# Strassen's scheme for three of the four kinds of products of an attention and two-layer kernel

## The chip, the cores and the metric

The kernel runs on one core of a Trainium2 chip. The metric is device time in microseconds (us); lower is better. The core's engines are TensorE (PE in the profile, with its weight loads as PEld), VectorE (DVE), ScalarE (ACT), GpSimd (POOL) and SyncE (SP, which only issues transfers here). Each runs its own instructions in order; they wait for each other with semaphores.

## The reference

Chunk-local softmax attention over 8 batches, 8 heads, 576 tokens and a head size of 64, in chunks of 64 tokens; its output, as 4608 tokens of 512 numbers, goes through two layers:

```python
scores = scale * np.matmul(q_c, k_c.transpose(0, 1, 2, 4, 3))
attn = softmax(scores)
x = np.matmul(attn, v_c)            # as [4608, 512]
g = x @ w_gate                      # [4608, 1536]
silu = g * (1.0 / (1.0 + np.exp(-g)))
x = silu * (x @ w_val) @ w_out      # [4608, 512]
h = x @ w_in                        # [4608, 2048]
g = h * (1.0 / (1.0 + np.exp(-1.702 * h)))
out = g @ w_out2                    # [4608, 512]
```

The weights reach the kernel as the bits of float64 numbers.

## The kernel before

**Tiles.** The tokens are cut into nine blocks of 512 (four units of 128 each). d_ff is cut into tiles of 128: 12 in layer 1, 16 in layer 2. A float32 operand is split into a high and a low part of float32r (`split`: ScalarE copies the high part, VectorE or GpSimd subtracts it to get the low one), and each product is three matmuls, high by high, high by low and low by high (`mm3`, lines 211 to 214). All operands of the layers stand in SBUF in both parts.

**Stages.** Phase 1 takes the blocks through attention and layer 1, with all of layer 1's weights on chip (36 tiles of 4 KB a partition, tag `w`). For each f tile there are a gate product and a value product (`product`, 4 k tiles x 3 = 12 matmuls of 512 columns each), then `gate` and `times` on ScalarE and VectorE, `split_h`, and one tile later `y_step`: 12 matmuls into four PSUM banks that gather the block's output. The block's y goes to DRAM. Blocks 0 and 1 share the time in which weights arrive: block 0 runs through half of d_ff, block 1 through all of it, then block 0 through the rest. In the first two f tiles the products are made in halves of 256 tokens. Phase 2 loads y back (`y_load`) and takes the blocks through layer 2 in the same way (`product`, `gate`, `split_h`, `o_step`, whose matmuls are lines 422 to 424); a block has 192 matmuls in its input products and 192 in `o_step`. One block thus has 288 + 144 matmuls in layer 1 and 192 + 192 in layer 2.

**Weights.** `conv_part` turns float64 words into float32 with one ScalarE instruction and three on VectorE (lines 266, 269, 272), and `split` makes the parts, the low one on GpSimd. `conv_to` spreads this over the first 200 us and over the last block of phase 1, where layer 2's weights take the place of layer 1's.

**Attention** (`attend`) on a unit: 32 small matmuls, a maximum, eight exponentials, a sum, a reciprocal and a product with it, four transposes, 32 small matmuls (lines 304 to 337). Units are made ahead of the block that needs them, over all of phase 1.

**Order.** Every instruction group is an `op` with a rough duration and a priority (a slot number). `Program.emit` is a list scheduler over these durations: it fixes, before the kernel runs, the order of each engine's instructions; the op with the lowest priority goes first among those that could start soonest. All transfers are issued by SP in the order so found, loads at line 200 and stores at line 203.

## Time and profile before

| what | value |
|---|---|
| time, median of 3 runs | 1839.46 us (1839.08 to 1840.76) |
| span of the profiled execution | 1837.8 us |
| the profiled execution's own time | not given beside its span |
| TensorE busy | 1818.9 us (99%), 9920 matmuls |
| VectorE, ScalarE, GpSimd busy | 741.6, 627.5, 109.7 us |
| transfers | 94.37 MB on SP's queue, 51 GB/s over the span |

The span runs from the first to the last instruction of one profiled execution. Busy shares say how long an engine had some instruction in flight. The chain that ended last is followed back from the last instruction through whatever released each one. Tables of stretches give the busy time of every engine between two times, the granted TensorE clock as a fraction of 2.4 GHz and the transfers' share and rate.

### The profile page before, as it was taken

The page shows a single profiled execution, that of the slowest core. Times are in us where ns is not written, and L with a number is a line of the kernel's source. Part 1 is how long each engine was busy: PE and PEld are TensorE (multiplying, and loading weights), DVE is VectorE, ACT ScalarE, POOL GpSimd, SP SyncE. Part 2 cuts the span into 40 slices and gives each one's busy share as a digit, 9 for nine tenths or more (in the row PEclk, how much of TensorE's full clock was granted, in tenths as well). Part 3 has the DMA queues.
Part 4 walks back from the last instruction along what each step waited for, and adds up shares of the span by engine and source line. Part 5 has one row for each costly group of instructions (what it writes and reads, how often), then busy time and mean ns, then how long its engine had stood idle before and what let it go on. Part 6 is the DMA issues. An engine that isn't in the chain of part 4 may idle for free.

```text
span 1837.8 us, 24124 instructions
## 1 busy us (share of the span) xinstructions
PE 1818.9 (99%) x9920; PEld 1476.0 (80%) x9920; DVE 741.6 (40%) x1246; ACT 627.5 (34%) x1208; POOL 109.7 (6%) x117
## 2 busy tenths in 40 slices
PE   8999999999999999999999999999999999999999
PEld 7777888888888878887888778888888888888887
DVE  7886333333333333333358863232323232323222
ACT  6663333233333332332335542222222222222222
POOL 2442000000000000000013320000000000000000
PEclk9999999999999999999999999999999999999999
DMA  8511121011101111011023521010101010100000
GB/s 327 207 41 41 58 63 42 24 58 29 46 30 35 46 29 50 32 29 47 29 92 125 162 80 47 0 47 0 46 1 47 1 46 1 46 1 35 1 23 24
DMA packets 47342, 95.91 MB, mean 52 GB/s; under 512 B 5248, under 2 KB 14464, under 8 KB 47232
## 3 DMA queue, kind: packets, MB, share of 16 engines
q1 hardware_dynamic: 47232, 94.37, 15.4%
q8 instruction: 78, 1.28, 0.3%
q14 instruction: 32, 0.26, 0.0%
HBM read 74.42 MB, written 19.92 MB: 51 GB/s over the span
## 4 chain that ended last, share of the span: by engine, by line
PE 84%; DVE 7%; issue 3%; ACT 3%; DMA 2%; POOL 0%; DVEq 0%; SPq 0%; ACTq 0%; POOLq 0%
PE g L212 16%; PE g L213 15%; PE g L214 15%; PE y L424 7%; PE y L423 7%; PE y L422 7%; PE y L212 5%; PE y L214 4%; PE y L213 4%; PE a L304 3%; DVE t L269 2%; DVE t L272 2%; DVE raw L266 1%; ACT t L264 1%; DMA w<-in_moe_w_val 1%
## 5 line engine op out<-in xcount | busy, mean ns | idle before, releaser
L363 DVE TENSOR_TENSOR h<-h,g 128x512 f32<-128x512 f32 x358 | 245.8, 686 | 753.4 <-ACT h L366 662.1
L366 ACT ACTIVATE h<-g 128x512 f32<-128x512 f32 x251 | 150.0, 598 | 643.8 <-PE g L214 643.1
L212 PE MATMUL g<-xbh,w 128*128 128x512 f32 x736 | 289.0, 393 | 0.8 <-DVE h L363 0.7
L213 PE MATMUL g<-xbl,w 128*128 128x512 f32 x736 | 287.6, 391 | 0.1
L214 PE MATMUL g<-xbh,w 128*128 128x512 f32 x736 | 286.6, 389 | 0.0
L212 PE MATMUL g<-xah,w 128*128 128x512 f32 (+1 forms) x704 | 279.4, 397 | 0.0
L214 PE MATMUL g<-xah,w 128*128 128x512 f32 (+1 forms) x704 | 277.7, 394 | 0.0
L213 PE MATMUL g<-xal,w 128*128 128x512 f32 (+1 forms) x704 | 277.5, 394 | 0.0
L206 ACT CAST hh<-h 128x512 fp32r<-128x512 f32 x252 | 156.4, 621 | 266.1 <-DVE h L363 265.7
L424 PE MATMUL y<-w,hl 128*128 128x512 f32 x576 | 229.2, 398 | 0.9 <-DVE hl L209 0.9
L422 PE MATMUL y<-w,hh 128*128 128x512 f32 x576 | 224.5, 390 | 1.5 <-DVE e L380 1.5
L423 PE MATMUL y<-w,hh 128*128 128x512 f32 x576 | 225.6, 392 | 0.0
L209 DVE TENSOR_TENSOR hl<-h,hh 128x512 fp32r<-128x512 f32 x246 | 169.7, 690 | 126.8 <-ACT hh L206 126.3
L212 PE MATMUL y<-hh,w 128*128 128x512 f32 x432 | 175.2, 406 | 0.2 <-PE y L457 0.2
L213 PE MATMUL y<-hl,w 128*128 128x512 f32 x432 | 169.9, 393 | 0.0
L214 PE MATMUL y<-hh,w 128*128 128x512 f32 x432 | 169.9, 393 | 0.0
L212 PEld LDWEIGHTS g<-xbh,w 128*128 128x128 f32 x736 | 138.1, 188 | 32.8 <-DVE h L363 2.4
L214 PEld LDWEIGHTS g<-xbh,w 128*128 128x128 f32 x736 | 138.2, 188 | 29.6
L213 PEld LDWEIGHTS g<-xbl,w 128*128 128x128 f32 x736 | 138.2, 188 | 29.5 <-DVE xbl L209 0.4
L212 PEld LDWEIGHTS g<-xah,w 128*128 128x128 f32 x704 | 132.9, 189 | 31.5 <-DVE h L363 0.5
L209 POOL TENSOR_TENSOR w<-t,w 128x256 fp32r<-128x256 f32 (+1 forms) x104 | 100.1, 964 | 968.8 <-ACT w L206 932.3
L214 PEld LDWEIGHTS g<-xah,w 128*128 128x128 f32 x704 | 132.9, 189 | 31.1
(84 smaller groups left out, 1645.7 us busy)
## 6 DMA issues: line engine op xcount, KB each, us to landing
e<-y_dram SPq DMA_DIRECT2D x36, 256.0 KB, 3.0
raw<-in_moe_w_out SPq DMA_DIRECT2D x36, 255.8 KB, 2.6
q<-in_q SPq DMA_DIRECT2D x32, 256.0 KB, 2.7
k<-in_k SPq DMA_DIRECT2D x32, 256.0 KB, 3.0
v<-in_v SPq DMA_DIRECT2D x32, 256.0 KB, 2.8
raw<-in_moe_w_in SPq DMA_DIRECT2D x32, 255.8 KB, 2.6
y_dram<-raw SPq DMA_DIRECT2D x28, 256.0 KB, 2.4
w<-in_moe_w_gate SPq DMA_DIRECT2D x11, 511.8 KB, 7.5
```

The costliest lines, as they stand in the source:

```text
L206: op("act", ((61 if psum else 112) + n) / 1.2e3, lambda: nc.scalar.copy(out=hi.ap, in_=src.ap), [src], [hi], prio)
L209: op(eng, us, lambda: e.tensor_tensor(out=lo.ap, in0=src.ap, in1=rd(hi.ap), op=ALU.subtract), [src, hi], [lo], prio)
L212: nc.tensor.matmul(o, ah, bh, start=first, stop=False)
L213: nc.tensor.matmul(o, ah, bl, start=False, stop=False)
L214: nc.tensor.matmul(o, al, bh, start=False, stop=last)
L269: op("dve", (66 + n) / 0.96e3, lambda: nc.vector.scalar_tensor_tensor(out=t.ap.bitcast(I32), in0=t.ap, scalar=-4096 * up, in1=word(1).bitc ...
L304: nc.tensor.matmul(o[r, of_o(i)], st[r, of_st(i)], mv[r, of_o(i)], start=True, stop=True)
L363: op("dve", 0.61, lambda: nc.vector.tensor_tensor(out=h.ap, in0=h.ap, in1=g.ap, op=by), [h, g], [h], prio)
L366: op("act", 0.48, lambda: nc.scalar.activation(out=h.ap, in_=g.ap, func=AF.Sigmoid, scale=by), [g], [h], prio, "sig")
L422: nc.tensor.matmul(os_[t].ap, gh.ap[:, ts], wh.ap, start=first, stop=False)
L423: nc.tensor.matmul(os_[t].ap, gh.ap[:, ts], wl.ap, start=False, stop=False)
L424: nc.tensor.matmul(os_[t].ap, gl.ap[:, ts], wh.ap, start=False, stop=last)
```

## The change

The two layers are done in five passes over all nine blocks: three for layer 1 (4 of its 12 f tiles each) and two for layer 2 (8 of 16). A pass has two groups of f tiles. For a group, the gate and value products (layer 1: two f tiles, so a 512 x 256 weight block for each of the two) or the input products (layer 2: four f tiles, as two such blocks) are made by Strassen's scheme, one level, in Winograd's form with seven products: the weight block and the block's x (512 x 512 tokens) are each cut in two both ways, and seven combinations of either side are multiplied, 12 matmuls of 256 columns for each combination and group. The seven partial products are added up on VectorE into `c`. The products with `wo` and `wo2` (`second`) stay as they were, 12 matmuls of 512 columns for each f tile.

What goes with it:

- Combinations of x: in pass 0 they are made from attention's output (`x_made`, four VectorE sums, seven splits on ScalarE and GpSimd) and stored to DRAM with both parts; passes 1 and 2 load them (`x_load`, seven tiles of 4 KB a partition for each block). In pass 2, y is summed up and its combinations are made and stored in the same way (`x_to_dram`) for passes 3 and 4.
- Combinations of weights (`combos`, four GpSimd sums of 256 columns): the first pass makes them from the host's weights at the start; during each pass those of the next one are converted, combined, split and stored to DRAM (`group_to_dram`), and loaded at the change of the pass (`pass_from_dram`). The ring `w` has 24 tiles; a pass takes 18 or 22.
- `conv_part` has two ScalarE instructions and two on VectorE in place of one and three.
- The low part of h is always made on GpSimd (`gated`); before, VectorE made it but for the first slots.
- y of layer 1, and now the output of layer 2 too, is summed over the passes through DRAM (`block_sum`).
- All attention runs in pass 0, block by block, with one buffer each for q, k, v, its scores and its second PSUM bank. PSUM: in pass 0 the partial products have two banks, later four.
- `second`'s matmuls of a group are put between the next group's products (`put`). The planner's durations are set anew.

The diff, cut to its core:

```diff
-        ("w", 3 * NF1), ("xah", 1), ("xal", 1), ("xbh", 1), ("xbl", 1), ("h", 1), ("hh", 2), ("hl", 2),
...
+        ("w", 24), ("x", 8), ("c", 3), ("s1", 1), ("u", 1), ("h", 2), ("hh", 3), ("hl", 3),
+        ("q", 1), ("k", 1), ("v", 1), ("e", 2), ("m", 2), ("z", 2), ("xr", 1), ("xt", 3),
+        ("raw", 2), ("t", 3), ("st", 3), ("ws", 2), ("yv", 2))}
...
+        ("y0", 1), ("y1", 1), ("y2", 1), ("y3", 1), ("g", 2), ("s", 1), ("a", 1))})
...
+                if layer == 1:
+                    g.pairs = [[wg[f] for f in fs], [wv[f] for f in fs]]
+                    g.outs = [wo[f] for f in fs]
+                    g.name = "a%d" % fs[0]
+                else:
+                    g.pairs = [[wi[f] for f in fs[:2]], [wi[f] for f in fs[2:]]]
+                    g.outs = [wo2[f] for f in fs]
+                    g.name = "b%d" % fs[0]
...
+        op("act", act_us(n), lambda: nc.scalar.activation(
+            out=t.ap, in_=raw.ap[:, :, 2], func=AF.Relu, scale=up, bias=offset.ap[:, :1]), [raw, offset], [t], prio)
+        op("act", act_us(n), lambda: nc.scalar.activation(
+            out=word(1).bitcast(F32), in_=raw.ap[:, :, 2], func=AF.Relu, scale=up, bias=offset.ap[:, 1:]),
+           [raw, offset, t], [raw], prio)
...
+    def combos(t0, t1, prio):
+        def half(i):
+            return lambda ap: ap[:, i * 256:(i + 1) * 256]
+        s1, s2, s3, s4 = [ring["st"].new([P, 256]) for _ in range(4)]
+        a = half(0), half(1)
+        yield t0, a[0]
+        yield t0, a[1]
+        tt(s1, t1, t1, ALU.add, 256, prio, "pool", a[0], a[1])
+        tt(s2, s1, t0, ALU.subtract, 256, prio, "pool", of_b=a[0])
+        yield s2, lambda ap: ap
+        tt(s3, t0, t1, ALU.subtract, 256, prio, "pool", a[0], a[0])
+        yield s3, lambda ap: ap
+        yield s1, lambda ap: ap
+        tt(s4, t0, s2, ALU.subtract, 256, prio, "pool", of_a=a[1])
+        yield s4, lambda ap: ap
+        yield t1, a[1]
...
+    def group_from_host(g, prio):
+        W[g] = [ring["w"].new([P, 2, 2, 256], F32R) for _ in range(7)], [ring["w"].new([P, 2, 512], F32R) for _ in g.fs]
+        ts = []
+        for var in range(2):
+            ts.append([conv_tile((g.name, var, i), g.pairs[var][i], prio) for i in range(2)])
+            for i, (src, cut) in enumerate(combos(*ts[-1], prio)):
+                hi, lo = [W[g][0][i].part(lambda ap, c=c, var=var: ap[:, var, c]) for c in range(2)]
+                split(hi, lo, src, 256, prio + 0.1 * i, "pool", cut)
...
+    def token_combos(xb, prio):
+        def quarter(j, n):
+            return lambda ap: ap[:, 2 * j:2 * j + 2, n * HT:(n + 1) * HT]
+        b = [[quarter(j, n) for n in range(2)] for j in range(2)]
+        t1, t2, t4 = [ring["xt"].new([P, 2, HT]) for _ in range(3)]
+        tt(t1, xb, xb, ALU.subtract, 512, prio, of_a=b[0][1], of_b=b[0][0])
+        tt(t2, xb, t1, ALU.subtract, 512, prio, of_a=b[1][1])
+        t3 = Buf(lambda: b[0][1](xb.ap), None, None, xb)
+        op("dve", dve_us(512), lambda: nc.vector.tensor_tensor(
+            out=t3.ap, in0=b[1][1](xb.ap), in1=b[0][1](xb.ap), op=ALU.subtract), [xb, t1], [t3], prio)
+        tt(t4, t2, xb, ALU.subtract, 512, prio, of_b=b[1][0])
+        same = lambda ap: ap
+        return [(xb, b[0][0]), (xb, b[1][0]), (t2, same), (t3, same), (t1, same), (xb, b[1][1]), (t4, same)]
...
+    def x_made(b, prio):
+        X[0, b] = []
+        for i, (src, cut) in enumerate(token_combos(xr.pop(b), prio)):
+            x = ring["x"].new([P, 2, 2, HT], F32R)
+            X[0, b].append(x)
+            split(*[x.part(lambda ap, c=c: ap[:, c]) for c in range(2)], src, 512, prio + i, "pool" if b else ("dve", "pool")[i % 2], cut)
+            store(x_dram[0][:, b, i], Buf(lambda x=x: x.ap.rearrange("p c a t -> p c (a t)"), None, None, x), [xd[0][b][i]], prio + i + 2)
...
+    def x_load(p, b, prio):
+        layer = passes[p][0]
+        X[p, b] = []
+        for i in range(7):
+            x = ring["x"].new([P, 2, 2, HT], F32R)
+            X[p, b].append(x)
+            load(x.part(lambda ap: ap.rearrange("p c a t -> p c (a t)")), x_dram[layer - 1][:, b, i], prio + 2 * i, [xd[layer - 1][b][i]])
...
+    def x_to_dram(xb, b, prio):
+        for i, (src, cut) in enumerate(token_combos(xb, prio)):
+            hi, lo = [ring[t].new([P, 2, HT], F32R) for t in (("q", "k"), ("v", "e"))[i % 2]]
+            split(hi, lo, src, 512, prio + i, "pool", cut)
+            for c, s in enumerate((hi, lo)):
+                store(x_dram[1][:, b, i, c], Buf(lambda s=s: s.ap.rearrange("p a t -> p (a t)"), None, None, s), [xd[1][b][i].part(None)], prio + i + 2)
...
+            m_tags.extend(["g", "g"] if prio < start[1][0] else ["g", "s", "g", "a"])
+        m = ring[m_tags.pop(0)].new([P, 2, HT])
+        w, x = W[g][0][i], xs[i]
+        def fn():
+            for var in range(2):
+                for kk in range(2):
+                    ks, cs = slice(kk * P, kk * P + P), kk
+                    mm3(m.ap[:, var], w.ap[:, var, 0, ks], w.ap[:, var, 1, ks], x.ap[:, 0, kk], x.ap[:, 1, kk],
+                        kk == 0, kk == 1)
+        op("pe", GV, fn, [w, x], [m], prio)
+        return m
...
+        for i in range(7):
+            at_i = at(i)
+            m = product(g, xs, i, at_i)
+            if i == 0:
+                copy(s1, m, 512, at_i)
+            elif i == 1:
+                tt(q[0][0], s1, m, ALU.add, 512, at_i)
+            elif i == 2:
+                tt(u2, s1, m, ALU.add, 512, at_i)
+            elif i == 3:
+                tt(u3, u2, m, ALU.add, 512, at_i)
+            elif i == 4:
+                tt(q[0][1], u2, m, ALU.add, 512, at_i)
+                tt(q[1][1], u3, m, ALU.add, 512, at_i)
+            elif i == 5:
+                tt(q[0][1], q[0][1], m, ALU.add, 512, at_i)
+            else:
+                tt(q[1][0], u3, m, ALU.subtract, 512, at_i)
+            put(i)
+        return c
...
+        for i, var in ([(0, 0), (1, 0)] if g.layer == 1 else [(i, var) for var in range(2) for i in range(2)]):
+            h = ring["h"].new([P, 2, HT])
+            by = 1.0 if g.layer == 1 else 1.702
+            op("act", act_us(512), lambda h=h, i=i, var=var, by=by: nc.scalar.activation(
+                out=h.ap, in_=of(var)(c[i].ap), func=AF.Sigmoid, scale=by), [c[i]], [h], prio, "sig")
+            tt(h, h, c[i], ALU.mult, 512, prio, of_b=of(var))
+            if g.layer == 1:
+                tt(h, h, c[i], ALU.mult, 512, prio, of_b=of(1))
+            hh = ring["hh"].new([P, BT], F32R)
+            hl = ring["hl"].new([P, BT], F32R)
+            split(*[Buf(lambda s=s: s.ap.rearrange("p (n t) -> p n t", n=2), s.prev, s.before, s) for s in (hh, hl)],
+                  h, 512, prio, "pool")
+            hs.append((hh, hl))
...
+            s = ring["yv"].new([P, BT])
+            copy(s, ys[e], 512, prio, "act" if e % 2 else "dve")
+            yd[layer, b, e] = Buf(None)
+            store(dram, s, [yd[layer, b, e]], prio)
+            return
...
+        s = ring["yv"].new([P, BT])
+        load(s, dram, prio - 14, [yd[layer, b, e]])
+        if last and layer == 1:
+            if e == 0:
+                xr[b] = ring["xr"].new([P, KD, BT])
+            tt(xr[b].part(lambda ap: ap[:, e]), s, ys[e], ALU.add, 512, prio)
+            if e == KD - 1:
+                x_to_dram(xr.pop(b), b, prio + 3)
+            return
...
+                def put(i, tj=tj, n=n, step=step):
+                    while len(pend) > n * (6 - i) // 7:
+                        pend.pop(0)(tj + (i + 0.5) * step / 7)
+                c = group_products(g, xs, lambda i, tj=tj, step=step: tj + i * step / 7, put)
...
+                if p == 0 and b + 1 < NB:
+                    for u in range(2):
+                        w = UPB * (b + 1) + 2 * j + u
+                        at = t + (2 * j + u) * 7
+                        attend(w, "s", at, at - 10)
+                    if j == 1:
+                        x_made(b + 1, start[p][b + 1] - 12)
...
```

## Rows read from the trace of the kernel before

**Rows 1.** The page: busy time by engine, and the chain by engine.
```profile
PE 1818.9 (99%) x9920; PEld 1476.0 (80%) x9920; DVE 741.6 (40%) x1246; ACT 627.5 (34%) x1208; POOL 109.7 (6%) x117
...
PE 84%; DVE 7%; issue 3%; ACT 3%; DMA 2%; POOL 0%; DVEq 0%; SPq 0%; ACTq 0%; POOLq 0%
```

**Rows 2.** Table of stretches: us, busy by engine, granted clock, DMA share, GB/s.
```profile
200.00:400.00 200.00, 200.00 (x1339) 162.00 (x1338) 76.56 (x133) 72.38 (x146) 0.00 (x0) 1.00 0.16 52
```

**Rows 3.** Timeline of SP: a block's first output store, eight blocks apart.
```profile
1127.46 0.34 SPq L203 DMA_DIRECT2D out<-raw  x1
...
1832.89 0.33 SPq L203 DMA_DIRECT2D out<-raw  x1
```

**Rows 4.** Timeline of SP: first stores of y, block 0's second half and block 8.
```profile
270.38 0.92 SPq L203 DMA_DIRECT2D y_dram<-t  x2
...
1039.59 0.80 SPq L203 DMA_DIRECT2D y_dram<-e  x2
```

**Rows 5.** Timeline of PE: 256-column matmuls, in two products the third and the twelfth.
```profile
24.35 0.28 PE L214 MATMUL g<-xah,w 128*128 128x256 f32 x1
...
25.41 0.28 PE L214 MATMUL g<-xah,w 128*128 128x256 f32 x1
...
27.43 0.28 PE L214 MATMUL g<-xah,w 128*128 128x256 f32 x1
...
28.50 0.28 PE L214 MATMUL g<-xah,w 128*128 128x256 f32 x1
```

**Rows 6.** Timeline of PE: 512-column matmuls from the same x buffer, twenty starts apart.
```profile
204.07 0.39 PE L212 MATMUL g<-xah,w 128*128 128x512 f32 x1
...
208.73 0.39 PE L214 MATMUL g<-xah,w 128*128 128x512 f32 x1
```

**Rows 7.** Groups by shape: weight loads, busy us and mean ns of one.
```profile
L212 PEld LDWEIGHTS g<-xah,w 128*128 128x128 f32 x704 | 132.9, 189 | 31.5 <-DVE h L363 0.5
```

**Rows 8.** Groups by shape: elementwise work, busy us, mean ns of one, idle before.
```profile
L363 DVE TENSOR_TENSOR h<-h,g 128x512 f32<-128x512 f32 x358 | 245.8, 686 | 753.4 <-ACT h L366 662.1 <-PE g L214 87.2
L206 ACT CAST hh<-h 128x512 fp32r<-128x512 f32 x252 | 156.4, 621 | 266.1 <-DVE h L363 265.7
L366 ACT ACTIVATE h<-g 128x512 f32<-128x512 f32 x251 | 150.0, 598 | 643.8 <-PE g L214 643.1 <-POOL hl L209 0.4
L209 POOL TENSOR_TENSOR w<-t,w 128x256 fp32r<-128x256 f32 x72 | 56.1, 779 | 885.9 <-ACT w L206 854.3 <-issue 24.9 <-POOL w L209 3.4
L209 POOL TENSOR_TENSOR w<-t,w 128x512 fp32r<-128x512 f32 x32 | 44.1, 1380 | 82.9 <-ACT w L206 78.0 <-DMA w<-in_moe_w_gate 5.0
L272 DVE SCALAR_TENSOR_TENSOR t<-raw,t 128x256 int32<-128x256 int32 x72 | 39.8, 553 | 2.1
L312 DVE TENSOR_REDUCE m<-a 128x8 f32<-128x512 f32 x32 | 22.0, 689 | 9.6 <-PE a L304 9.6
```

**Rows 9.** Timelines of DVE and POOL: a small op alone, and one beside GpSimd.
```profile
58.11 0.17 DVE L323 TENSOR_SCALAR z<-z 128x8 f32<-128x8 f32 x1
...
73.47 1.28 DVE L323 TENSOR_SCALAR z<-z 128x8 f32<-128x8 f32 x1
...
73.43 1.29 POOL L209 TENSOR_TENSOR hl<-h,hh 128x512 fp32r<-128x512 f32 x1 [2.67 <-ACT hh L206]
```

**Rows 10.** Groups of VectorE by shape, from 50 to 120 us alone.
```profile
L272 DVE SCALAR_TENSOR_TENSOR t<-w,t 128x512 int32<-128x512 int32 x17 | 14.0, 828 | 0.3
...
L323 DVE TENSOR_SCALAR z<-z 128x8 f32<-128x8 f32 x3 | 2.6, 863 | 0.1
...
L313 DVE TENSOR_SCALAR m<-m 128x8 f32<-128x8 f32 x4 | 1.8, 438 | 0.0
```

**Rows 11.** Table of stretches as in rows 2: saturated loads, and a loaded VectorE.
```profile
25.00:30.00 5.00, 5.00 (x87) 4.60 (x87) 4.53 (x8) 3.58 (x7) 1.55 (x2) 1.00 1.04 402
50.00:120.00 70.00, 64.96 (x443) 51.72 (x440) 58.20 (x91) 46.46 (x84) 28.68 (x21) 0.98 0.44 162
```

**Rows 12.** Timeline of POOL: its first work on weights.
```profile
9.04 1.27 POOL L209 TENSOR_TENSOR w<-t,w 128x512 fp32r<-128x512 f32 x1 [7.69 <-ACT w L206]
```

More of the change, by code (lines that the diff above doesn't have):

```diff
@@ L259, in conv_part @@
-    def conv_part(raw, t, n, need):
+    class Group:
+        pass
+    passes = []
+    for layer, nf, per in ((1, NF1, 4), (2, NF2, 8)):
+        for f0 in range(0, nf, per):
+            gs = []
+            for j in range(2):
+                g = Group()
+                fs = list(range(f0 + j * per // 2, f0 + (j + 1) * per // 2))
+                g.fs = fs
+                if layer == 1:
[6 more added lines that the diff above has]
+                    g.name = "b%d" % fs[0]
+                g.layer = layer
+                gs.append(g)
+            passes.append((layer, gs))
@@ new lines, in attention_two_moe_kernel, with conv_load @@
+    NPASS = len(passes)
+    GV, YS = 1.42, 0.70
+    start = []
+    t = 0.0
+    for p, (layer, gs) in enumerate(passes):
+        start.append([])
+        for b in range(NB):
+            start[p].append(t)
+            t += sum(7 * GV + 4 * YS * len(g.fs) for g in gs) + (10.5 if p == 0 and b < NB - 1 else 0)
+    start.append([t])
+    raws = {}
+    def conv_load(key, src, prio, early):
+        src = src.bitcast(I16)
+        n = 1 if early else 2
+        raws[key] = [ring["w" if early else "raw"].new([P, 512 // n, 4], I16) for i in range(n)]
+        for i, raw in enumerate(raws[key]):
+            w = 2048 // n
+            load(raw.part(lambda ap, w=w: ap.rearrange("p c t -> p (c t)")[:, :w - 1]), src[:, i * w + 1:(i + 1) * w],
+                 prio, width=2)
@@ L260, in word, with conv_tile, conv_part @@
+    def conv_tile(key, src, prio):
+        if key not in raws:
+            conv_load(key, src, prio - 8, False)
+        t = ring["t"].new([P, 512])
+        rs = raws.pop(key)
+        n = 512 // len(rs)
+        for i, raw in enumerate(rs):
+            conv_part(raw, t.part(lambda ap, c=i * n: ap[:, c:c + n]), n, prio)
+        return t
+    def conv_part(raw, t, n, prio):
         def word(i):
@@ L432, in attention_two_moe_kernel @@
[L432 to L445 removed]
+        copy(xr[b].part(lambda ap: ap[:, :, ts]), o, 512, prio, cut=lambda ap: ap.rearrange("p (a t) -> p a t", a=NP))
@@ new lines, in second, with fn @@
+    def second(layer, w, hh, hl, ys, e, first, last, prio):
+        es = slice(e * P, (e + 1) * P)
+        def fn():
+            if layer == 1:
+                mm3(ys[e].ap, w.ap[:, 0, es], w.ap[:, 1, es], hh.ap, hl.ap, first, last)
+            else:
+                mm3(ys[e].ap, hh.ap[:, es], hl.ap[:, es], w.ap[:, 0], w.ap[:, 1], first, last)
+        op("pe", YS, fn, [w, hh, hl], [ys[e]], prio)
+    y_dram = pool["dram"].tile([P, KD, NT], F32, name="y_dram")
+    o_dram = pool["dram"].tile([P, KD, NT], F32, name="o_dram")
@@ L545, in attention_two_moe_kernel @@
-    o_step(*pend, slot)
+        op("pe", 0.22, lambda: nc.tensor.matmul(warm.ap[:, :P], ident.ap, ident.ap, start=True, stop=True), [warm], [], 9999)
+    g0, g1 = passes[0][1]
+    early = [((g.name, var, i), g.pairs[var][i]) for g in (g0, g1) for var in range(2) for i in range(2)]
+    for j, (key, src) in enumerate(early[:EARLY]):
+        conv_load(key, src, -52 + 2 * j, True)
+        raws[key][0].ap
+    tags = ("g", "s", "y1", "y2")
+    for u in range(UPB):
+        attend(u, tags[u], -40 + 4 * u, -54 + 4 * u)
@@ new lines, in attention_two_moe_kernel, with spread, flush @@
+    group_from_host(g0, -22)
+    x_made(0, -15)
+    outs_from_host(g0, 2)
+    group_from_host(g1, 0)
+    outs_from_host(g1, 8)
+    def spread(p):
+        if p + 1 >= NPASS:
+            return []
+        jobs = [j for g in passes[p + 1][1] for j in group_to_dram(g, 0)]
+        a = start[p][0] + (45 if p == 0 else 10)
+        z = start[p + 1][0] - 60
+        return [(a + (z - a) * i / len(jobs), j) for i, j in enumerate(jobs)]
+    pend = []
+    def flush(n):
+        for _ in range(min(n, len(pend))):
+            pend.pop(0)()
```

403 lines of the change are left out of this document (166 added, 237 removed).

## The prediction, made before the changed kernel was run

> **What bounds the kernel now.** The page's table of engines comes first: TensorE is busy 99% of the span, VectorE 40%, ScalarE 34%, GpSimd 6%, and the chain that ended last gives TensorE 84% [rows 1]. A busy TensorE need not be a working one, since matmuls overlap, so the table of stretches is next: from 200 to 400 us it is busy 200.00 of 200 us at granted clock 1.00, the 2.4 GHz level, with VectorE at 38% [rows 2]. There only fewer or cheaper matmuls can save time. Their rate comes from the output stores: the first store of a block is issued at 1127.46 us and that of the block eight later at 1832.89 [rows 3]. Between them stand 8 x 384 - 12 = 3060 matmuls of 512 columns (after the last block no next product is put ahead of its sums), so one takes 705.43 / 3060 = 0.2305 us. In layer 1 seven blocks lie between the two stores of [rows 4]: 769.2 us, of which 7 x 432 - 12 = 3012 matmuls take 694.3; the rest, 74.9 us, is 24 attention units, 3.12 us each.
>
> The span then splits so: 9 blocks x 816 = 7344 matmuls x 0.2305 = 1692.8 us; 32 attention units x 3.12 = 99.9 (the first block's four lie in the start); what is left, 45.1 us, is start and end.
>
> **Products.** Of the 816 matmuls of a block, 480 are gate, value and second-layer input products: 4320 in all, 995.8 us. Strassen makes seven block products of eight and cuts the moving side to 256 columns: 90 groups (five passes, nine blocks, two groups) x 7 x 12 = 7560 matmuls. The kernel before has 256-column matmuls of the same form in its first slots: nine starts apart take 1.06 us in one product and 1.07 in the next [rows 5], 0.1183 us each. In the same x buffer one of 512 takes (208.73 - 204.07) / 20 = 0.2330 [rows 6], so halving the columns costs 1.55% more per column, and on the kernel's mean rate a 256-column matmul comes to 0.2305 / 2 x 1.0155 = 0.117 us. 7560 x 0.117 = 884.5: a gain of 111.3 us. Nothing extra per column gives 871 (a gain of 125), the slower stretch's 0.1189 gives 899 (97); I take the scaled value, since the x tiles come to lie in eight buffers and not in that one.
>
> The rule that speaks against this: the Trainium skill ("TensorE: Matmul & The Clock Gate", Part 3, The mechanism) has a weight load run beside a matmul only where their row groups differ, and here every load takes all rows. By that rule a pair would cost load plus matmul, and the change would lose far more than it gains. The trace disagrees: loads that last 189 ns in the records [rows 7] stand between matmuls 118 ns apart.
>
> **Second products and attention** keep their count: 3024 x 0.2305 = 697.0 and 99.9 us. With 884.5 that is 1681.4, and with the old 45.1 for start and end 1726.5 us: the span if everything added is hidden.
>
> **What is added beside TensorE.** Each group now evacuates seven partial products: one copy on ScalarE, seven 128x512 adds on VectorE; then the gate (ScalarE), two products per h in layer 1 (VectorE), the high part (ScalarE) and the low part, which moves from VectorE to GpSimd. By rows a VectorE op of this size is 0.69, ScalarE 0.60 to 0.62, GpSimd 1.38, or 0.78 for 256 columns [rows 8]. Half a block of layer 1 gives TensorE 84 x 0.117 + 24 x 0.2305 = 15.4 us, of layer 2 20.9. So a block has 30.7 us in pass 1 and 2, 43.2 in pass 0 (four attention units more) and 41.8 in pass 3 and 4.
>
> VectorE in pass 0, per block: 22 group ops 15.2, attention 4 x 2.7 = 10.8 (three ops of 0.69 and three of 0.2), four sums for Strassen's x 2.8, two copies of y 1.4, a ninth of the next pass's weight conversion (12 tiles x 4 x 0.55) 2.9: 33.1 of 43.2. In pass 2: 15.2, four sums of y and four of x 5.5, a ninth of 16 tiles 3.9: 24.6 of 30.7. In pass 1 it is 21 of 30.7, in 3 and 4 under 21 of 41.8. GpSimd, which did 6% of the span, gets two low parts 2.8 x 2, seven x splits 9.7 and a ninth of some 52 weight ops 4.5 in pass 0, 19.8 of 43.2 (46%), and 20.5 of 30.7 (67%) in pass 2.
>
> Those two cannot run freely side by side. A VectorE scalar op on 8 columns takes 0.17 us when GpSimd is idle; the one at 73.47 us takes 1.28, to the end of the GpSimd subtraction that began at 73.43 [rows 9]. Between 50 and 120 us, GpSimd busy 41% and VectorE 83% [rows 11], the shift of the weight conversion (two SBUF operands) averages 0.83 and the small scalar ops 0.86 and 0.44 [rows 10], against 0.69 and 0.2. Scaled to GpSimd's share, 0.16 x 21 + 0.5 x 8 = 7 us make VectorE 40 of 43.2 in pass 0, and 0.22 x 19 = 4.3 make it 28.9 of 30.7 in pass 2: still under TensorE, but with little left. Lower: 0, as in [rows 2] at a third of the load. Upper: TensorE's idle share of 50 to 120 us, 5.04 of 70 us or 7.2% [rows 11], on the 8 x 43.2 + 9 x 30.7 = 622 us of these two passes: 45. And the chain behind a group's last product (0.69 + 0.60 + 2 x 0.69 + 0.62 + 1.38 = 4.7 us) is covered by a leftover second product and two products, about 4: at worst 0.6 x 90 = 54 more. I take 28 of 99: the 50 to 120 us stretch also waited for weights that were still coming, and the planner puts more products into a gap that it foresees.
>
> The Trainium skill ("SBUF — State Buffer", Who interferes with whom) says that a VectorE op with two SBUF inputs, or in a two-port mode, and a GpSimd op that reads SBUF exclude each other entirely. By that alone pass 2 would hold the pair for 19 x 0.6 + 20.5 = 32 of 30.7 us and end 12 us later. The trace agrees on the exclusion, but what remains of a held VectorE op after GpSimd's end is short.
>
> **Transfers.** All go through SP's queue, in order. Loads saturate at 402 GB/s [rows 11]. Pass 2 asks most per block: seven x tiles of 0.52 MB, four y loads and fourteen x stores of 0.26 MB and a ninth of 16 weight tiles in and 44 halves out: 10.6 MB in 30.7 us, 345 GB/s, 86%. Pass 1 asks 245, the others less. Where a pass ends, seven weight tiles and seven x tiles (7.3 MB, 18.3 us at 402) meet in a half block of 15.4: up to 3 us, four times; I take 8 in all (0 to 12).
>
> **Start and end.** GpSimd begins on weights at 9.04 us [rows 12] and has 44 ops of 256 and 18 of 512 columns, 59 us, before block 1: done by 68 if fed, where the sum starts that block at about 83. But it waited for most of its start before, and the single q, k and v buffers now string block 0's four units: 10 us (0 to 60). At the end the last group's chain is bare: 4 us, which the second products before it now hide.
>
> **Sum.** 1726.5 + 28 + 8 + 10 + 4 = 1776.5 us of span. The page has no time but the span; the runs' median lies 1.7 us above it: **1778 us**, 3.3% faster. What a measurement here can tell from no change is about 0.2%, 3.7 us.
>
> **Rivals.** *All hidden* (0.14): 1726.5 + 1.7 = 1728. For: VectorE ops that follow each other start 0.6 apart and not 0.69, so the loads above are high. Against: [rows 11]. *GpSimd holds VectorE* (0.18, slower): if every held op waits 0.73 us, two thirds of 1.1 as in the 1.28 of [rows 9], pass 0 needs 33.1 + 29 x 0.73 = 54 of 43.2 and pass 2 24.6 + 19 x 0.73 = 38 of 30.7: 8 x 11 + 9 x 7.5 = 156, so 1726.5 + 22 + 156 + 1.7 = 1906. It decides from about 0.56 us per op, where the sum passes 1839; the mean seen is 0.14 for the most and 0.24 to 0.69 for the small ones. *Queue* (0.09): if stores and waits on SP leave 300 GB/s, pass 2 takes 35.3 us a block and each change of pass 24 us for 15: 9 x 4.6 + 4 x 9 = 77 on 1756 (the forecast without its 8 and half of its 28): some 1835, about no change. *Loads bind* (0.02, slower): if weights cannot follow faster than their 189 ns, 7560 x 0.189 = 1429 instead of 884.5: some 2320; against it [rows 5]. The forecast has 0.57.
>
> **Numbers.** Faster are the forecast, *all hidden* and half of *queue*: 0.57 + 0.14 + 0.05 = 0.76. Same: 0.04 from *queue*. Slower: 0.20. The range runs from 1722, which takes in *all hidden* with some of its cheaper products, to 1860, past *queue* and into the lower end of the GpSimd case, where its waits are 0.61 us; it leaves out most of that case, the loads, and the best of the best.
>
> **What would show it.** Right: 256-column matmuls 0.115 to 0.119 apart; TensorE solid in pass 1, 3 and 4 with blocks of 31 and 42 us; its gaps in pass 0 and 2, released by VectorE adds, with VectorE near 90% and small scalar ops of 0.5 us and more. Wrong: pass 0 blocks over 50 us, pass 2 over 35, gaps that end on x tiles from DRAM, or a first block done long after 83 us.

## The result, and the profile after the change

The changed kernel takes **1856.16 us** (median of 4 runs, 1853.84 to 1857.77); the kernel before takes 1839.36. The ratio is 1.0088, 95% interval [1.0074, 1.0103]: slower by 0.9%, where 3.3% faster was forecast. The time lies inside the range, near its upper end.

From the page: busy times (they answer to [rows 1]), transfers, the chain by engine, and three of the landing times.

```profile
PE 1760.1 (95%) x13128; PEld 1585.6 (85%) x13128; DVE 1115.8 (60%) x1686; ACT 775.8 (42%) x1602; POOL 739.2 (40%) x654
...
DMA packets 174931, 414.32 MB, mean 223 GB/s; under 512 B 18736, under 2 KB 46896, under 8 KB 174768
...
PE 60%; DMA 18%; DVE 7%; POOL 6%; issue 5%; ACT 4%; SPq 1%; POOLq 0%; DVEq 0%; ACTq 0%
...
x<-x_dram SPq DMA_DIRECT2D x252, 512.0 KB, 4.9
...
yv<-y_dram SPq DMA_DIRECT2D x72, 256.0 KB, 4.0
...
w<-wd_a SPq DMA_DIRECT2D x28, 512.0 KB, 6.3
```

TensorE has less to do, 1760 us busy for 1819, and stands still for 96 us of the span. The bytes moved went from 95.91 to 414.32 MB. A transfer of 256 KB lands 3.4 to 4.0 us after its issue (medians of the groups above); in the kernel before it was 2.4 to 3.0:

```profile
e<-y_dram SPq DMA_DIRECT2D x36, 256.0 KB, 3.0
raw<-in_moe_w_out SPq DMA_DIRECT2D x36, 255.8 KB, 2.6
```

The timeline of SP, first store of a block's sums, dates the stages: pass 0, block 0 and block 8; the last block of pass 1; in pass 3 blocks 0, 2 and 8; the last block of pass 4.

```profile
117.20 0.32 SPq L222 DMA_DIRECT2D y_dram<-yv  x1
...
485.62 0.32 SPq L222 DMA_DIRECT2D y_dram<-yv  x1
...
783.92 0.33 SPq L222 DMA_DIRECT2D y_dram<-yv  x1
...
1131.34 0.80 SPq L222 DMA_DIRECT2D o_dram<-yv  x2
...
1215.24 0.92 SPq L222 DMA_DIRECT2D o_dram<-yv  x2
...
1469.24 0.91 SPq L222 DMA_DIRECT2D o_dram<-yv  x2
...
1845.96 0.34 SPq L222 DMA_DIRECT2D out<-yv  x1
```

Pass 3 is solid (TensorE waits next to nowhere in it): (1469.24 - 1215.24) / 6 = 42.33 us a block, where 41.8 were forecast. Pass 1 takes 298.3 / 9 = 33.1 us a block for the 30.7 of the forecast. In pass 0 the eight blocks take 368.4 us; four attention units more in seven of them make 8 x 30.7 + 28 x 3.12 = 333 by the forecast. The table of stretches, in the middle of passes 1 and 2, has TensorE idle for 4% of each:

```profile
490.00:750.00 260.00, 249.26 (x1679) 228.59 (x1678) 169.18 (x264) 96.19 (x192) 95.20 (x97) 0.98 0.80 272
800.00:1060.00 260.00, 248.49 (x1705) 228.50 (x1705) 195.99 (x265) 95.79 (x179) 139.64 (x108) 0.99 0.87 293
```

Waits of TensorE from 485 to 1131 us (us in total, times, longest):

```profile
PE y L241 <- POOL hl L233: 20.1, 17, 3.1
```

Waits of ScalarE over the span:

```profile
ACT t L315 <- DMA raw<-in_moe_w_out: 60.2, 22, 9.6
ACT ws L226 <- DMA wd_b<-ws: 51.3, 26, 5.7
ACT t L315 <- DMA raw<-in_moe_w_in: 39.3, 17, 7.3
ACT q L226 <- DMA x_dram<-q: 34.4, 12, 5.2
```

A second product waits for the low part of h, which GpSimd makes. ScalarE, which makes the high part ahead of it, has stood behind transfers: raw weights not yet landed, staging tiles whose store is not yet done. One such wait in pass 1, by the chain that ended last: the store of a staging tile takes 6.43 us, GpSimd's work on the next staged weights comes behind it in the order, then the low part of h, and only then the second product.

```profile
671.41 6.43 DMA wd_b<-ws
...
678.40 0.72 POOL ws L233
679.12 0.66 POOL st L233
...
680.22 1.73 POOL hl L233
681.99 0.79 PE y L241
```

So there were two theories. **A**: GpSimd's 1.36 us for the low part makes the chain late. **B**: the planner is wrong. `emit` counts 0.74 us per 256 KB on the queue and 2.0 us from there to landing, 2.74 in all, which fits the kernel before and not this one; so it puts work that waits for transfers ahead of work that TensorE needs. A third, **C**, was for the rate: the address of an operand sets it.

### The profile page after: what moved, and what is told of

The parts are those of the page before. It is cut to its first block, busy times and chain, and to the rows that moved or that the text cites. A ratio compares the mean times of both kernels' runs of the same rounds, so it can differ in the third digit from the quotient of the medians.

```text
span 1856.0 us, 34284 instructions
## 1 busy us (share of the span) xinstructions
PE 1760.1 (95%) x13128; PEld 1585.6 (85%) x13128; DVE 1115.8 (60%) x1686; ACT 775.8 (42%) x1602; POOL 739.2 (40%) x654
## 2 busy tenths in 40 slices
DMA packets 174931, 414.32 MB, mean 223 GB/s; under 512 B 18736, under 2 KB 46896, under 8 KB 174768
## 4 chain that ended last, share of the span: by engine, by line
PE 60%; DMA 18%; DVE 7%; POOL 6%; issue 5%; ACT 4%; SPq 1%; POOLq 0%; DVEq 0%; ACTq 0%
PE y L241 9%; PE y L240 9%; PE y L242 9%; PE g L240 6%; PE g L241 6%; PE g L242 6%; DMA x_dram<-k 3%; DVE h L233 2%; PE s L242 2%; PE s L240 2%; PE s L241 2%; PE a L240 2%; PE a L242 2%; PE a L241 2%; POOL hl L233 2%
## 5 line engine op out<-in xcount | busy, mean ns | idle before, releaser
L233 POOL TENSOR_TENSOR hl<-h,hh 128x512 fp32r<-128x512 f32 x252 | 340.6, 1358 | 731.7 <-ACT hh L226 631.2
L241 PE MATMUL g<-x,w 128*128 128x256 f32 x1512 | 430.3, 285 | 9.9 <-POOL x L233 9.8
L240 PE MATMUL g<-x,w 128*128 128x256 f32 x1512 | 433.9, 287 | 5.6 <-ACT x L226 2.7
L242 PE MATMUL g<-x,w 128*128 128x256 f32 x1512 | 428.4, 283 | 0.0
L233 DVE TENSOR_TENSOR h<-h,c 128x512 f32<-128x512 f32 x360 | 307.9, 865 | 106.3 <-ACT h L585 103.0
L585 ACT ACTIVATE h<-c 128x512 f32<-128x512 f32 x252 | 158.6, 631 | 492.1 <-DVE c L233 473.2
L241 PEld LDWEIGHTS g<-x,w 128*128 128x128 f32 x1512 | 287.4, 190 | 23.4 <-POOL x L233 13.2
L240 PEld LDWEIGHTS g<-x,w 128*128 128x128 f32 x1512 | 287.5, 190 | 21.8 <-ACT x L226 3.3
L242 PEld LDWEIGHTS g<-x,w 128*128 128x128 f32 x1512 | 287.4, 190 | 0.0
L241 PE MATMUL y<-hl,w 128*128 128x512 f32 x432 | 177.3, 411 | 25.4 <-POOL hl L233 25.1
L240 PE MATMUL y<-hh,w 128*128 128x512 f32 x432 | 177.5, 411 | 9.6 <-ACT hh L226 7.5
L242 PE MATMUL y<-hh,w 128*128 128x512 f32 x432 | 173.5, 402 | 0.0
L233 DVE TENSOR_TENSOR c<-u,g 128x512 f32<-128x512 f32 x162 | 106.5, 682 | 70.1 <-PE g L242 68.5
L242 PE MATMUL a<-x,w 128*128 128x256 f32 x504 | 142.3, 282 | 0.0
L240 PE MATMUL a<-x,w 128*128 128x256 f32 x504 | 142.3, 282 | 0.0
L241 PE MATMUL a<-x,w 128*128 128x256 f32 x504 | 142.3, 282 | 0.0
L242 PE MATMUL s<-x,w 128*128 128x256 f32 x504 | 142.2, 282 | 0.0
L241 PE MATMUL s<-x,w 128*128 128x256 f32 x504 | 142.2, 282 | 0.0
```

The costliest lines, as they stand in the source:

```text
L233: lambda: e.tensor_tensor(out=dst.ap, in0=of_a(a.ap), in1=of_b(b.ap), op=by), [a, b], [dst], prio)
L240: nc.tensor.matmul(o, ah, bh, start=first, stop=False)
L241: nc.tensor.matmul(o, ah, bl, start=False, stop=False)
L242: nc.tensor.matmul(o, al, bh, start=False, stop=last)
L585: op("act", act_us(512), lambda h=h, i=i, var=var, by=by: nc.scalar.activation(out=h.ap, in_=of(var)(c[i].ap), func=AF.Sigmoid, scale=by), ...
```

## The experiments

### A or B

```diff
-                  h, 512, prio, "pool")       # e1: in gated
+                  h, 512, prio, "dve")
-            end = free[o.eng] + (2.0 if o.eng == "dma" else 0.0)     # e2: in emit
+            end = free[o.eng] + (4.0 if o.eng == "dma" else 0.0)
```

**e1.** 

> Only edit: the low part of h (h minus its rounded copy) is made by VectorE instead of GpSimd. Theory A (the chain behind a group's last product is late because GpSimd needs 1.36 us for the low part, in order behind its other work): pass 1 falls from 33.1 to about 31.5 us a block and pass 2 from 33.3 to about 32, pass 0 by 5 to 20 us, in all 1815 to 1835 us. Theory B (ScalarE and GpSimd stand behind transfers that land later than the order of work assumes, and pass that on): the waits stay, now ended by VectorE or ScalarE, and the time stays at 1848 to 1862 us. Passes 3 and 4 move by less than 3 us under both. A third way: VectorE, 76% busy in pass 0, takes 252 more operations of 0.7 to 0.9 us and pass 0 grows by 10 us or more.

Measured: 1870.45 us, ratio 1.0158 [1.0132, 1.0185]. A falls. The waits of passes 1 and 2 are still there, now ended by other engines:

```profile
PE y L241 <- DVE hl L233: 11.0, 18, 1.2
PE y L240 <- ACT hh L226: 9.3, 9, 2.3
```

Pass 0 grew by 17 us (the third way) and pass 1 by 1; pass 2 gained 5.

**e2.** 

> Only edit: the planner that fixes the order of each engine counts 4.0 us instead of 2.0 us from a transfer's end on its queue to its landing (measured: 3.4 to 6.3 us). The instructions are the same, only their order on each engine changes. Theory B: ScalarE's waits on weight tiles and on stores (60 + 39 + 51 + 34 us) fall to half, and passes 0 to 2 give back 20 to 40 us: 1815 to 1836 us. Theory A: the waits of ScalarE fall too, but the low parts stay as late as before; 1848 to 1860 us.

Measured: **1804.47 us** (1804.26 to 1804.65), ratio 0.9807 [0.9793, 0.9822]: 51.7 us less than the changed kernel, from one number, with the same operations. The stretches that answer to those above (each pass now starts earlier):

```profile
490.00:750.00 260.00, 260.00 (x1807) 241.81 (x1806) 182.92 (x280) 97.03 (x192) 95.94 (x99) 1.00 0.85 294
760.00:1020.00 260.00, 259.82 (x1797) 241.06 (x1796) 210.28 (x288) 107.57 (x203) 159.19 (x127) 1.00 0.94 324
```

TensorE's only wait from 475 to 1082 us, by the list of waits:

```profile
PE y L240 <- ACT hh L226: 0.4, 1, 0.4
```

And the stages, by the stores of SP's timeline as above (without block 2 of pass 3):

```profile
117.86 0.42 SPq L222 DMA_DIRECT2D y_dram<-yv  x1
...
474.38 0.32 SPq L222 DMA_DIRECT2D y_dram<-yv  x1
...
754.90 0.32 SPq L222 DMA_DIRECT2D y_dram<-yv  x1
...
1081.94 0.90 SPq L222 DMA_DIRECT2D o_dram<-yv  x2
...
1420.53 0.91 SPq L222 DMA_DIRECT2D o_dram<-yv  x2
...
1792.75 0.34 SPq L222 DMA_DIRECT2D out<-yv  x1
```

Passes 1 and 2 are solid, with more transfers per us than in the changed kernel and GpSimd making every low part. Against the changed kernel pass 0 gave back 11.9 us, pass 1 17.8, pass 2 (to the first store of pass 3) 20.4, pass 4 4.5. ScalarE's waits on raw weights for the output products fell from 60.2 to 13.8.

One lucky order does not explain this. Ten runs have 4.0 for all transfers (e2, and e4 and e10 to e17 below, each with a further edit): pass 1 takes 280.2 to 281.6 us in each of them, by the same stores. In the four with 2.0 (the changed kernel, e1 and the two e3) it takes 295.1 to 299.4. But 4.0 is not the measured landing time either: it makes 4.74 us of a transfer of 256 KB, more than the 3.4 to 4.0 of the changed kernel's page, and 5.48 of one of 512 KB, where that page has 4.1 to 6.3. No other value was tried.

### Which transfers

`e5`, `e6`, `e8` and `e9` give the 4.0 to one kind of transfer and 2.0 to the rest, in this form:

```diff
+            end = free[o.eng] + (o.late if o.eng == "dma" else 0.0)   # late: 4.0 for the kind tried, 2.0 for the rest
```

**e5.** 

> The changed kernel, with the planner's landing time at 4.0 us for the loads of raw weights alone (the loads that ScalarE's conversion waits for, 99.5 us of its idle time in the changed kernel), 2.0 us for all other transfers. If the raw weights are what blocks ScalarE and, behind it, the high and low parts of h: most of the 51 us come back, 1805 to 1820 us, and the waits of TensorE on the low parts in passes 1 and 2 fall from 20 us to under 5. If the stores of the staging tiles or the x loads do it: 1840 to 1858 us.

**e6.** 

> The complement: landing time 2.0 us for the loads of raw weights, 4.0 us for all other transfers. If the raw loads block: 1840 to 1858 us, and ScalarE still waits about 100 us on them. If the stores of staging tiles and the x tiles do: 1805 to 1820 us. If both take part: both runs lie between, about 1820 to 1840 us.

**e8.** 

> The changed kernel with the planner's landing time at 4.0 us for stores to DRAM alone (staging tiles ws, x, the high and low parts of the second layer's x, partial sums), 2.0 us for every load. If engines that stand behind a staging tile still in flight are the cause (ScalarE waits 51 + 23 + 34 us on stores, GpSimd 18): 1805 to 1825 us. If late loads of x and of weights from DRAM are: 1840 to 1858 us.

**e9.** 

> The complement: 4.0 us for every load (raw weights, prepared weights, x, partial sums, q, k, v), 2.0 us for stores. If loads are the cause: 1805 to 1825 us; if stores are: 1840 to 1858 us. If each needs the other (as raw loads alone gave nothing and the rest alone gave 33 of 51 us): both stay above 1820.

| 4.0 us for | time, us | ratio to before | against 1856.16 | pass 1, us | pass 2, us |
|---|---|---|---|---|---|
| none (the changed kernel) | 1856.16 | 1.0088 [1.0074, 1.0103] | 0 | 298.3 | 347.4 |
| raw weights (e5) | 1855.95 | 1.0096 [1.0078, 1.0114] | -0.2 | 289.2 | 345.5 |
| all others (e6) | 1823.34 | 0.9919 [0.9904, 0.9934] | -32.8 | 285.5 | 333.3 |
| stores (e8) | 1837.96 | 0.9990 [0.9981, 0.9999] | -18.2 | 283.6 | 342.9 |
| loads (e9) | 1836.67 | 0.9980 [0.9970, 0.9991] | -19.5 | 289.4 | 338.2 |
| all (e2) | 1804.47 | 0.9807 [0.9793, 0.9822] | -51.7 | 280.5 | 327.0 |

(Pass 1 and 2 by the first stores of sums, as above.)

In e5 ScalarE waits 6.4 us on `raw<-in_moe_w_out`, a tenth of the 60.2, and the whole time stays; e6 wins most with those waits unchanged (61.6). But e5 is not without effect: its pass 1 is 9.1 us shorter and its pass 2 1.9, while its first sum leaves at 125.15 us instead of 117.20 and takes that back. So the raw loads can't be acquitted; the new order of the start hides what they give in pass 1. Stores and loads carry some 19 us each and together 14 more: each needs the other, as the third case of e9 had it. So B is shown for the planner's landing time as a whole; which single wait costs most is not settled.

**e7** puts the same 4.0 into the kernel before. 

> The kernel before, with landing time 4.0 us instead of 2.0 us in its planner: what Strassen's scheme is worth under the better order. Before, TensorE stood still for some 45 us at start and end and next to nowhere else, so there is nothing for a better order to win: 1833 to 1845 us. If instead its 512-column rate of 0.2305 us hides stalls: 1800 to 1825 us, and the scheme is worth little under either order.

Measured: 1839.72 us, ratio 1.0007 [0.9998, 1.0017]. The kernel before had nothing to win; under one planner Strassen's scheme is worth 1839.72 - 1804.47 = 35 us.

### The rate

```diff
+    pad = fixed([P, 32], F32, "pad")     # e3_pad128; [P, 24] in e3_pad96
     ident = fixed([P, P], F32, "ident")
```

> Only edit: 128 unused bytes ahead of all SBUF tiles, so that the byte addresses modulo 256 become 160 for x, hh and hl (from 32) and 32 for w (from 160). In the kernel before, products that read the x buffer at 160 modulo 256 stood 0.2267 us apart and those that read the one at 32 stood 0.2333 us apart. If the address of the streamed operand sets this: 256-column products go from 0.1187 to about 0.1155 us, a block of pass 3 from 42.34 to 41.2 to 41.6 us, and the whole by 25 to 45 us (1810 to 1830). If the rate has nothing to do with addresses: pass 3 stays at 42.3 us a block and the time within 3 us of 1856.

> As the pad of 128 bytes, but 96 bytes: x, hh and hl stand at 128 and w at 0 modulo 256. If the rate depends on whether rows of 64, 128 or 256 bytes are cut by the operand's address: 256-column products at 0.115 us or less and a block of pass 3 at 41.2 us or less, faster than with 128 bytes. If only the half of 256 bytes matters (160 and 128 alike): as with 128 bytes. If addresses don't matter: pass 3 at 42.3 us a block, 1856 us within 3.

Measured: 1851.62 us (1.0073 [1.0053, 1.0092]) and 1855.11 (1.0086 [1.0061, 1.0111]). With 128 bytes, pass 3 from block 2 to block 8:

```profile
1209.67 0.33 SPq L223 DMA_DIRECT2D o_dram<-yv  x1
...
1463.67 0.32 SPq L223 DMA_DIRECT2D o_dram<-yv  x1
```

254.00 us, to the hundredth what it was, and with 96 bytes 254.00 again. C falls, if the pads moved the tiles as worked out; no trace shows addresses. The 4.5 us that the whole is shorter with 128 bytes are more than the 3 expected, and they don't come from pass 3. Why the kernel before had two rates, one for each x buffer, stays open.

### The start

```diff
+        if u < 3:      # e4: q, k in an x tile, v, e in a c tile
+            pairs = [ring["x"].new([P, 2, 2, HT], F32R), ring["c"].new([P, 2, 2, HT])]
```

> Against the version with landing time 4.0 (1804.5 us): the first three attention units take their q, k, v and e from tiles of the x and c rings that are still empty, instead of one buffer each of q, k and v. If the single buffers string block 0's attention (first product at 43.9 us, in the kernel before at 23.9 us): first product at 33 to 38 us, and the whole 1794 to 1800 us. If ScalarE's weight conversion in the same stretch (about 31 us busy in the first 44) bounds it: first product within 2 us of 43.9, 1802 to 1807 us.

Measured: 1818.40 us (0.9888 [0.9871, 0.9904]). The first product came at 40.52 us instead of 43.90, but the first sum left at 119.4 instead of 117.9, and pass 0 took 15 us longer. Neither theory foresaw that: the new buffers changed the order of everything after them.

### Pass 0

Under the best order pass 0 still takes (445.36 - 117.86) / 7 = 46.8 us a block. From the solid stretches a block's products need 31.14 (pass 1 of e2, (754.90 - 474.38) / 9 = 31.17, with one wait of 0.4), so with four units at 3.12 some 43.6. What holds it was sought by leaving work out of e2 or moving it (first sum of block 0; us a block from there to block 7):

| run | edit on e2 | first sum | us a block | time, us |
|---|---|---|---|---|
| e2 | none | 117.9 | 46.8 | 1804.47 |
| e10 | group 1 of pass 0 uses group 0's weights | 101.5 | 48.7 | 1804.00 |
| e11 | planner: 0.82 us for products that make h | 116.2 | 47.6 | 1812.14 |
| e12 | no weights made for pass 1 | 113.9 | 48.3 | 1816.41 |
| e13 | every second low part of x on VectorE | 115.7 | 49.5 | 1822.35 |
| e14 | attention stops after its scores, from block 1 on | 98.2 | 37.9 | 1726.60 |
| e15 | 10 x tiles, 22 weight tiles | 116.3 | 47.0 | 1805.97 |
| e16 | x due 20 us ahead, not 12 | 119.2 | 48.9 | 1820.31 |
| e17 | and attention due earlier | 113.3 | 48.8 | 1814.73 |

**e10.** The early loads of group 1's weights are left out as well (`EARLY`, 6 before, is 4).

```diff
-    group_from_host(g1, 0)
-    outs_from_host(g1, 8)
+    W[g1] = W[g0]
...
```

> On the version with 4.0 us for all (1804.5 us): the preparation of the second expert group's weights in block 0 of pass 0 is left out (the second group uses the first group's tiles, so its part of the output is not the reference's). Block 0 runs there from 43.9 to 117.9 us, 74 us against 43.7 us by its products and attention. If that preparation on ScalarE and GpSimd stretches block 0: the first partial sum leaves at 90 to 100 us and the whole takes 1778 to 1788 us. If the attention chain of block 1 and the split of its x stretch it: 112 to 118 us, 1798 to 1806 us.

**e11.** The same edit also stands at the other product.

```diff
-                tt(h, h, c[i], ALU.mult, 512, prio, of_b=of(1))
+                tt(h, h, c[i], ALU.mult, 640, prio, of_b=of(1))
```

> On the version with 4.0 us for all (1804.5 us): the planner also counts 0.82 us instead of 0.69 us for VectorE's products that make h (measured 0.86 us on average, two operands in SBUF). If the remaining loss of pass 0 (some 7 to 13 us) comes from this wrong duration: 1792 to 1800 us. If it is only another order of the same quality: 1800 to 1815 us.

**e12.** Pass 1 takes the tiles `W` of pass 0 and loads none.

```diff
-        jobs = spread(p)
+        jobs = spread(p) if p else []
...
```

> On the version with 4.0 us (1804.5 us): the preparation of pass 1's weights during pass 0 and their loads are left out; pass 1 uses pass 0's weight tiles (its part of the output is not the reference's). If that preparation is what holds pass 0 at 46.8 us a block (first partial sums of blocks 0 to 7): blocks of 43.7 to 44.5 us and 1780 to 1788 us in all. If attention or the x chain holds it: blocks of 46 us or more, 1797 to 1806 us.

**e13.**

```diff
-  "pool" if b else ("dve", "pool")[i % 2], cut)
+  ("dve", "pool")[i % 2], cut)
```

> On the version with 4.0 us (1804.5 us): in all blocks, as in block 0, every second low part of x is made by VectorE instead of GpSimd (GpSimd needs 1.28 us for each, in order behind the low parts of h). If the GpSimd chain ahead of each block holds pass 0: 44 to 45.5 us a block, 1785 to 1797 us. If VectorE's load does (80% busy in pass 0): blocks grow, 1805 to 1825 us.

**e14.** In `attend`, from unit 4 on, after the scores (v is not loaded either):

```diff
+            copy(xr[b].part(lambda ap: ap[:, :, ts]), s, 512, prio, cut=lambda ap: ap.rearrange("p (a t) -> p a t", a=NP))
+            return
```

> On the version with 4.0 us (1804.5 us): from block 1 on, attention stops after the scores, which are copied as x (softmax, transposes and the product with v are left out, so the output is not the reference's). TensorE's own work falls by about 2 us a unit, 28 units, 55 us; VectorE's by about 3.3 us and ScalarE's by 2.3 us a unit. If the attention chain or the load it puts on VectorE and ScalarE makes the excess of pass 0: blocks of 35.5 to 37 us (their own products then need 35.7), and 1715 to 1735 us. If not, the excess of 3 us a block stays: 38.5 to 40 us a block and 1740 to 1752 us.

**e15.**

```diff
-    ("w", 24), ("x", 8)
+    ("w", 22), ("x", 10)
```

> On the version with 4.0 us (1804.5 us): 10 x tiles instead of 8 and 22 weight tiles instead of 24. With 8 tiles and 7 to a block, the next block's x can only be made as the last products free them, and only after their store has been read. If that reuse holds pass 0: 44 to 45.5 us a block and 1785 to 1797 us, unless the weight tiles are late at the pass changes, which would show as gaps there. If not: 1800 to 1812 us.

**e16**, and **e17** with the second pair of lines as well:

```diff
-                        x_made(b + 1, start[p][b + 1] - 12)
+                        x_made(b + 1, start[p][b + 1] - 20)
-                        at = t + (2 * j + u) * 7
+                        at = t + (2 * j + u) * 6 - 6
```

> On the version with 4.0 us (1804.5 us): in pass 0 the combinations and the split of the next block's x are due 20 us ahead of the block instead of 12. If the place in the order holds pass 0: blocks of 44.5 to 46 us, 1788 to 1800 us. If the load of the softmax on VectorE and ScalarE does: 47 to 49 us a block, 1800 to 1815 us.

> As the run before, and the four attention units of a block are due at -6, 0, 6 and 12 us from its start instead of 0, 7, 14 and 21. If units and x chain together come too late: 43.7 to 45 us a block, 1780 to 1795 us. If the load holds it: 47 us or more, 1800 to 1820 us.

The preparation of group 1's weights does make block 0 late: without it the first sum leaves 16.3 us earlier. But the time doesn't move; by block 7 the lead is 445.36 - 442.13 = 3.2 us. In e12 the weights theory falls: with less work pass 0 is slower, and the whole takes 10 us more than the other theory allowed. The reuse of x tiles (e15) is not the cause either, nor are the due dates by themselves (e16, e17), and a better duration for VectorE (e11) made a worse order. The blocks of e13, e16 and e17 are as long as the load theory of each had them. Only e14 comes near its floor: from block 4 (254.27) to block 7 (363.33) 36.4 us a block, where its own products and scores need 31.14 + 4 x 1.15 = 35.7; the mean over seven is 37.9, an excess of 2.2 against 3.2 in e2.

What TensorE stands on in pass 0 of e2 is in its list of waits from 118 to 474 us, 18.7 us in all. The two largest are the low part of h, and attention's transposes, which wait for the softmax's last product on VectorE:

```profile
PE y L241 <- POOL hl L233: 7.7, 8, 1.5
PE a L473 <- DVE e L465: 5.8, 4, 3.8
```

In e14, where the softmax is gone, the waits on the low part are down to 1.9 us. That points at the softmax; but since some orders with the same or less work differ by 2 us a block, it doesn't settle whether its load or its place in the order holds pass 0; that is open.

## Why the prediction was wrong

What the changed kernel loses against the forecast's span, 1856.0 - 1776.5 = 79.5 us, falls into three terms.

**Products, forecast 884.5 + 697.0.** A block of layer 2 is 168 matmuls of 256 columns and 96 of 512, one of layer 1 168 and 48; from 42.33 and 31.14 us a 512-column one takes 0.2331 and a 256-column one 0.1188. 7560 x 0.1188 + 3024 x 0.2331 = 1603: **21 us** over the forecast. The step that failed is the scaling by the kernel's mean rate: 0.117 over what [rows 5] show themselves, 0.1183 as their mean and 0.1189 in the second product (13.6 us), and 0.2305 over the 0.2330 of [rows 6] (7.9 us). It was chosen because x would lie in eight other buffers; the measured values are those of the rows.

**Start, forecast 45.1 + 10 + 4.** With 1603 + 99.9 = 1703 for products and attention, 153 us of the span are lost; the passes lose 75 of them (below), start and end 78, **19 us** over. The first product comes at 43.53 us, where [rows 5] have one under way at 24.35: some 20 us, of which the ten for the strung units are half. e4 shows that the single buffers are worth 3.4 us of it, so the cause that the forecast named was the smaller part. The first sum left at 117.20 us, where the forecast had block 1 starting at about 83: its own sign of a wrong start, "a first block done long after 83 us". e10 shows 16 us in block 0 for weights that the forecast had done "by 68 if fed"; some of that was in the old 45.1.

**Stalls, forecast 28 + 8.** Pass 0 loses 368.4 - 8 x 31.14 - 28 x 3.12 = 31.9 us, pass 1 298.3 - 280.3 = 18.0, pass 2 20.4 and pass 4 4.5 against e2: 75, **39 us** over, and 18 of it in pass 1, which was to be solid. Of the 38 us of passes 1 and 2 TensorE was idle for 24 (10.7 and 13.4); some 7 more are 44 matmuls that ran at the lower clock after four of the waits (see the section on the hardware); the rest is not split. The step that failed is the one that sized the stalls by each engine's load: VectorE 21 of 30.7 us in pass 1 was taken as room enough. The loads were about right (e2 is solid there, VectorE at 70%), but room is not order. The sign that the forecast named for its gaps, VectorE near 90% and its adds as what ends them, did not come: in pass 2 VectorE is at 75%, and most waits of passes 1 and 2 end on low parts, in the one followed above behind a transfer. "The planner puts more products into a gap that it foresees" was written without asking what it foresees; 2.0 us to landing was a good number at 52 GB/s over the span and a bad one at 223, and with 4.0 in its place passes 0, 1, 2 and 4 gave back 54.6 us. The forecast counted the new traffic as a share of the queue (86% in pass 2), never as latency in the plan. The chain of 4.7 us behind a group's last product was no cause in passes 1 and 2: e2 has it too and is solid there. That the time still lies inside the range is luck: its upper end was set for *queue* and a part of *GpSimd holds VectorE*, and neither is what happened.

**The rivals.** *GpSimd holds VectorE* gave the right sign by the wrong mechanism: it decides from 0.56 us a held operation, and the products that make h take 0.865 us on average against 0.686 alone [rows 8], 0.18 more. The Trainium skill ("SBUF — State Buffer", Who interferes with whom) has such a pair exclude each other entirely, which was worked out to 12 us more in pass 2. The runs agree on the lengthening, not on the price: with 4.0 us pass 2 is solid beside it (VectorE 210 and GpSimd 159 of 260 us busy). *Queue* fails: e2 moves 324 GB/s in the middle of pass 2, with one wait of 0.4 us in passes 1 and 2 together. *All hidden* is right for passes 1 to 4 under e2. *Loads bind* fails: 0.1188 us apart with loads of 0.19.

**What was right.** The number of matmuls; a 256-column matmul within the 0.115 to 0.119 us that were to show it; the direction, once both kernels have the planner at 4.0 (35 us faster, of the 61 forecast); pass 3 solid and pass 4 but for eight waits, 2.1 us in all; no wait at the changes of pass worth naming.

## What to carry to other kernels

When a change multiplies the transfers of a kernel whose order is planned ahead, measure the landing times again and let the planner allow for them before judging the change: here that one number was worth 52 us, three times the loss that the change showed. Load sums per engine can only say that a stage may be solid; whether in-order engines stand behind transfers is read from their own waits, not from TensorE's. And where a stage has a row of its own kind, take the row, not a value scaled from another.

The best version measured that does all the work is the changed kernel with 4.0 us in the planner, 1804.47 us, 1.9% faster than the kernel before.
